# Wave 0 reordered, the second half of wave 1 transposed by the DMA crossbar, wave 2's loads strung out behind it and its work two steps later, in a fused linear-attention and MLP kernel

## The chip, the cores and the metric

One core of one Trainium2 chip. The metric is the time of one execution on the device in microseconds (us). A profile's span is some 2 us shorter than the time of the same execution. Most executions of a kernel agree within about 1%; a state is given where a run fell out of line ("slow", more than 1.5% above the fastest of the same kernel).

## The reference

Linear attention with decay over blocks of 64 positions (4 batches, 8 heads, 768 positions, head size 64), then an MLP (512 to 2048 to 512, 3072 tokens) with a GELU in its sigmoid form. All inputs and the output are float32.

```python
for b in range(nb):
    sl = slice(b * block, (b + 1) * block)
    qb, kb, vb = (q[:, :, sl], k[:, :, sl], v[:, :, sl])
    intra = np.einsum('bhic,bhjc->bhij', qb, kb) * Dmask[None]
    intra = np.einsum('bhij,bhjd->bhid', intra, vb)
    inter = np.einsum('bhid,bhde->bhie', qb * lam_pow[None], kv_state)
    out[:, :, sl] = intra + inter
    kb_dec = kb * rev_pow[None]
    kv_state = lam_block[None, :, None, None] * kv_state + np.einsum('bhsd,bhse->bhde', kb_dec, vb)
# x: the heads side by side, (3072, 512)
h = x @ w_in
g = h * (1.0 / (1.0 + np.exp(-1.702 * h)))
return (g @ w_out).astype(np.float32)
```

## The kernel before

The tokens are worked off in six waves of 512. Waves 0 and 1 are cut into "units" (two batches and a pair of heads; the units of wave 1 come in two halves, A and B), waves 2 to 5 into pairs of heads. For each, k and q are scaled and cast to bf16 (the tile `kqs`, by DVE and POOL), transposed (`kq`), multiplied to scores (`ps_s`), masked, and turned into an output, which is transposed once more into `xT`, the input of the MLP's first matmul (`ps_h`). A KV state is carried from wave to wave.

A list of main work (MLP matmuls, 0.216 us for 512 columns) carries a clock; attention work is slotted in by time on that clock. This order is the order of the program; each engine works through its own part of it in that order.

```python
def u_turn(w, bl, p):                      # waves 0 and 1: transposed by TensorE
    t = ps.tile([P, 8, P], bf16, ...)
    for i in range(2):
        for j in range(2):
            nc.tensor.transpose(t_ps[w, bl, p][:, i, j, :], kqs_of[w, p][:, bl, i, j]..., ident)

def p_cast(w, p):                          # waves 2 to 5: cast, then transposed by the crossbar
    ...
    nc.sync.dma_start_transpose(out=kq_of[w, p]..., in_=kqs...)

def p_out(w, p):
    ...
    nc.scalar.copy(xs.rearrange("s b h d -> s h b d"), o)
    nc.sync.dma_start_transpose(out=xT(w)[:, p], in_=xs.rearrange("p b h d -> p (b h d)"))

# ... loads of waves 0 and 1 and of both weights are queued here, on SyncE (SP) ...
load_batches(2)                            # all 12 loads of wave 2, right behind them
pump()                                     # issues what the ring of staging buffers has room for

# ... wave 0: for each unit transposes, inter and out of an older unit, scores of the last ...

e = clock[0]                               # start of wave 0's second matmul
# ... 16 steps of wave 0's output ...
states(e - 7, 0, 1.6)
units1(e + 2, B_UNITS, 2, nc.scalar, nc.scalar)
e = clock[0]
# ... 8 steps of wave 1's second half, 16 steps of its output ...
full(e + 1, e + 7.6, 2, 2.4)               # wave 2: casts from e + 1, scores from e + 7.6
load_spread(e + 4, 3, 1.8)                 # wave 3's loads, one at a time
```

## Time and profile before

| | before |
|---|---|
| time, median (range) | 220.36 us (220.35 to 221.56) |
| span of the profiled execution | 218.7 us |
| TensorE busy | 207.8 us (95%) |
| TensorE's waits behind 24 us | 0.7 us in total at most for any one cause |
| first matmul of wave 2's MLP | 92.78 us, without a wait |

The page's rows of the 40 slices (5.5 us each), here the bytes moved, show one thing that the prediction passed over: between 44 and 66 us, the ninth to twelfth slices, the DMA engines move 200 to 276 GB/s. Most of these bytes are wave 2's loads (twelve of 256 KB, 3.1 MB of some 5.0).

```profile
GB/s 137 295 290 364 342 315 389 362 276 201 218 222 86 145 242 167 225 242 221 207 171 186 233 161 227 134 147 192 236 151 73 46 74 83 88 0 0 48 51 96
```

### The profile page before, as it was taken

Reading aid. Unit: us, or ns where it says so; the run is one execution under the profiler, and the core shown is the slowest. Engines: PE = TensorE matmul, PEld = TensorE weight load, DVE = VectorE, ACT = ScalarE, POOL = GpSimd, SP = SyncE. Lnnn points to the kernel's source line nnn. Section 1 sums busy time; section 2 is a strip of 40 time slices with the busy share of each in tenths; the row PEclk is TensorE's granted clock in tenths of the full one; section 3 lists DMA queues with packets and bytes.
Section 4 is the critical chain, followed back from the end, with each engine's and each line's share of the span. In section 5 each row is a group of like instructions: output and inputs, shape, how many; then the busy total and the mean of one; then the engine's idle time right before and its main releaser. Section 6 shows DMA issues by size and latency. Waiting matters only on the chain.

```text
span 218.7 us, 4482 instructions
## 1 busy us (share of the span) xinstructions
PE 207.8 (95%) x1745; PEld 108.6 (50%) x1772; DVE 105.2 (48%) x237; ACT 97.4 (45%) x203; POOL 30.3 (14%) x62
## 2 busy tenths in 40 slices
PE   7887999899999999999999999999999999999993
PEld 2454454574547755444554444544444454444452
DVE  2577736595316888193572294661484332100121
ACT  5476867773655611156611075611176420376000
POOL 8780052041021000004000040000040000000000
PEclk9999999999999999999999999999999999999999
DMA  4999999999994999999989979667973222200112
GB/s 137 295 290 364 342 315 389 362 276 201 218 222 86 145 242 167 225 242 221 207 171 186 233 161 227 134 147 192 236 151 73 46 74 83 88 0 0 48 51 96
DMA packets 96741, 40.15 MB, mean 184 GB/s; under 512 B 77136, under 2 KB 89680, under 8 KB 96720
## 3 DMA queue, kind: packets, MB, share of 16 engines
q1 hardware_dynamic: 96576, 39.86, 76.5%
q8 instruction: 14, 0.23, 0.4%
q14 instruction: 7, 0.06, 0.1%
q10 hardware_dynamic: 144, 0.00, 0.0%
HBM read 27.27 MB, written 6.29 MB: 153 GB/s over the span
## 4 chain that ended last, share of the span: by engine, by line
PE 84%; DVE 4%; ACT 4%; DMA 2%; issue 2%; SPq 1%; POOL 1%
PE ps_h L450 35%; PE ps_out L481 35%; PE ps_o L431 2%; PE ps_s L394 2%; DMA ring<-in_q_dram 2%; DVE w_out L150 2%; PE ps_out L497 2%; SPq L89 1%; ACT kv_bd L335 1%; PE ps_kv L409 1%; PE ps_o L369 1%; PE ps_o L424 1%; PE ps_t L280 1%; PE ps_o L360 1%; PE ps_s L301 1%
## 5 line engine op out<-in xcount | busy, mean ns | idle before, releaser
L450 PE MATMUL ps_h<-xT,w_in 128*128 128x512 bf16 (+1 forms) x438 | 87.1, 348 | 1.3 <-ACT g_sb L456 0.7
L456 ACT ACTIVATE g_sb<-ps_h 128x512 bf16<-128x512 f32 (+1 forms) x112 | 59.6, 536 | 57.6 <-PE ps_h L450 56.2
L481 PE MATMUL ps_out<-w_out,g_sb 128*128 128x512 bf16 x354 | 80.8, 379 | 0.8 <-issue 0.3
L450 PEld LDWEIGHTS <-w_in 128*128 128x128 bf16 x448 | 42.2, 98 | 38.5 <-issue 1.1
L481 PEld LDWEIGHTS <-g_sb 128*128 128x128 bf16 x368 | 34.8, 98 | 38.9
L488 DVE COPY o_sb<-ps_out 128x512 f32<-128x512 f32 x19 | 13.1, 691 | 52.6 <-PE ps_out L481 47.1
L401 DVE SCALAR_TENSOR_TENSOR sm<-ps_s,inv_pow,mask 128x512 bf16<-128x512 f32 x32 | 22.6, 747 | 22.9 <-PE ps_s L394 22.8
L383 POOL CAST v_sb<-ring 128x512 bf16<-128x512 f32 x16 | 9.8, 656 | 102.1 <-DMA ring<-in_v_dram 68.0
L434 ACT CAST xs<-ps_o 128x512 bf16<-128x512 f32 x16 | 9.4, 586 | 29.2 <-PE ps_o L431 29.2
L306 DVE TENSOR_TENSOR sm<-ps_s,mask 128x512 bf16<-128x512 f32 x16 | 11.0, 689 | 11.9 <-PE ps_s L301 11.9
L263 POOL TENSOR_TENSOR kqs<-ring,kq_pow 128x256 bf16<-128x256 f32 x16 | 10.3, 652 | 27.9 <-DMA ring<-in_q_dram 27.8
L413 DVE SCALAR_TENSOR_TENSOR kv<-kv,blk,ps_kv 64x256 bf16<-64x256 bf16 x24 | 11.4, 475 | 0.2
L381 DVE TENSOR_SCALAR kqs<-ring,k_pow 128x256 bf16<-128x256 f32 x32 | 11.2, 391 | 0.2
L381 DVE TENSOR_SCALAR kqs<-ring,q_pow 128x256 bf16<-128x256 f32 x32 | 11.1, 390 | 0.0
L288 ACT COPY kq<-ps_t 128x512 bf16<-128x512 bf16 x12 | 7.0, 586 | 9.1 <-PE ps_t L280 9.0
L255 PE MATMUL ps_f<-zeros 128*128 128x512 bf16 x25 | 9.3, 506 | 1.7 <-DVE zeros L178 1.3
L263 DVE TENSOR_TENSOR kqs<-ring,kq_pow 128x256 bf16<-128x256 f32 x16 | 7.5, 474 | 5.5 <-DMA ring<-in_k_dram 3.0
L350 DVE TENSOR_TENSOR kv<-kv_bd,ps_kv 64x128 bf16<-64x128 bf16 x16 | 4.6, 286 | 8.2 <-PE ps_kv L347 7.9
L371 ACT CAST xT<-ps_o 128x256 bf16<-128x256 f32 x16 | 6.0, 373 | 3.6 <-PE ps_o L369 3.5
L280 PEld LDWEIGHTS <-kqs 128*128 128x128 bf16 x64 | 4.7, 98 | 5.7 <-DVE kqs L263 1.9
L280 PE MATMUL ps_t<-ident,kqs 128*128 128x128 bf16 x64 | 6.4, 220 | 1.0 <-POOL kqs L263 0.7
L150 DVE CAST w_out<-ring 128x512 bf16<-128x512 f32 x16 | 7.1, 498 | 0.1
(66 smaller groups left out, 117.8 us busy)
## 6 DMA issues: line engine op xcount, KB each, us to landing
ring<-in_k_dram SPq DMA_DIRECT2D x23, 256.0 KB, 4.9
ring<-in_q_dram SPq DMA_DIRECT2D x23, 256.0 KB, 4.4
ring<-in_v_dram SPq DMA_DIRECT2D x23, 256.0 KB, 4.5
ring<-in_moe_w_in_dram SPq DMA_DIRECT2D x16, 256.0 KB, 5.9
ring<-in_moe_w_out_dram SPq DMA_DIRECT2D x16, 256.0 KB, 5.4
out_dram<-o_sb SPq DMA_DIRECT2D x15, 256.0 KB, 2.2
out_dram<-o_sb SPq DMA_DIRECT2D x18, 128.0 KB, 2.6
ring<-in_k_dram SPq DMA_DIRECT2D x2, 128.0 KB, 3.2
```

Of the source, the lines that this page charges most:

```text
L150: eng.tensor_copy((w_in_sb if kind == "in" else w_out_sb)[j][:, r, :], read(kind, j, r))
L263: eng.tensor_tensor(kqs_of[w, p][:, bl, i].rearrange("s j h d -> s h j d"), read(w, "kq"[i], bl, p), tab, op=MUL)
L280: nc.tensor.transpose(t_ps[w, bl, p][:, i, j, :], kqs_of[w, p][:, bl, i, j].rearrange("s h d -> s (h d)"), ident)
L306: nc.vector.tensor_tensor(sm.rearrange("s h j t -> s h (j t)"), s_ps.pop((w, bl, p))[:, :, 0 : 2 * P], mask2.to_broadcast([P, 2, 2 * P]), ...
L381: nc.vector.tensor_scalar(kqs[:, i, :, h, :], x[:, :, p, h, :], scalar1=(k_pow, q_pow)[i][:, 2 * p + h : 2 * p + h + 1], scalar2=None, op0 ...
L383: nc.gpsimd.tensor_copy(v_sb[w % 2][:, p], read(w, "v")[:, :, p])
L401: nc.vector.scalar_tensor_tensor(sm[:, h], s[:, h], inv_pow[:, 2 * p + h : 2 * p + h + 1], mask.to_broadcast([P, B, P]), op0=MUL, op1=MUL)
L413: nc.vector.scalar_tensor_tensor(new[hd(h), p], old[hd(h), p], blk2[hd(h), p : p + 1], t[hd(h), :, hd(h)], op0=MUL, op1=ADD)
L450: nc.tensor.matmul(t[:, bs[0] * P : bs[1] * P], w_in_sb[fc // CW][:, kc, (fc % CW) * P : (fc % CW + 1) * P], xT(w)[:, kc, bs[0] : bs[1], : ...
L456: nc.scalar.activation(g_tile(w)[:, fc, c], h_ps.pop((w, fc))[:, c], GELU)
L481: nc.tensor.matmul(t, g_of[w][:, fc, g * P : (g + 1) * P], w_out_sb[j][:, fc % CW, :], start=(fc == 0), stop=(fc == FFC - 1))
L488: nc.vector.tensor_copy(o, t)
```

## The change

Its intent: in the head, open the circle of waits in wave 0 (scores first, so that the scaling of the KV state isn't waited for), one filler matmul less a unit, the GELU table loaded early, some first loads issued by ACT, three slices of w_in cast by POOL. In wave 1's second half, take 16 transposes off TensorE. To keep the queue clear for those crossbar transposes, wave 2's loads are strung out behind them; and wave 2's casts and scores move two steps (1.7 us) later. The core of the diff, cuts marked:

```diff
+    for p in range(2):
+        load_units(0, "k", 0, p, 1)
+        load_units(0, "q", 0, p, 1, nc.scalar)
 ...
-    load_batches(2)
     pump()
 ...
+    nc.scalar.activation(warm, inv_pow[:, 0:1], GELU)      # the table, early
 ...
+    def u_xbar(w, bl, p):
+        nc.sync.dma_start_transpose(out=kq_of[w, p][:, bl]..., in_=kqs_of[w, p][:, bl]...)
 ...
-                nc.vector.tensor_copy(o[:, 0 : hw // 2], t[:, 0 : hw // 2])
-                nc.scalar.copy(o[:, hw // 2 :], t[:, hw // 2 :])
+                nc.scalar.copy(o, t)                       # the last half of the output
 ...
-    FILL0, FILL1 = 12, 2
+    FILL0, FILL1 = 12, 1
 ...
-        nc.gpsimd.memset(blk_bd, 0.0)                      # before the loop over units
+            if i == 1:                                     # in the loop, ahead of the casts
+                nc.gpsimd.memset(blk_bd, 0.0)
 ...
-            if u2:
-                u_inter(0, *u2)
-            if u:
-                u_turn_copy(0, *u, nc.scalar)
-            if u2:
-                u_out(0, *u2)
             if u1:
                 u_score(0, *u1)
                 u_kv0(0, *u1)
                 ...
+            if u2:
+                u_inter(0, *u2)
+                u_out(0, *u2)
 ...
+        def units1b(t_cast, t0, c_step, step):
+            for i in range(n):
+                at(t_cast + c_step * i, u_cast_kq, 1, 0, *u, nc.vector)
+                at(t_cast + c_step * i, u_cast_kq, 1, 1, *u, nc.gpsimd)
+                at(t_cast + c_step * i, u_xbar, 1, *u)
 ...
-        units1(e + 2, B_UNITS, 2, nc.scalar, nc.scalar)
+        units1b(e + 3.4, e + 8.5, 1.2, 1.6)
+        load_spread(e + 4, 2, 1.15)
 ...
-        full(e + 1, e + 7.6, 2, 2.4)
+        full(e + 3, e + 9.6, 2, 2.4)
```

More of the change, by code (lines that the diff above doesn't have):

```diff
@@ L84, with load_units @@
     head, used, where, coming = [0], set(), {}, []
-    def load_units(w, nm, bl, p, n=2):
+    def load_units(w, nm, bl, p, n=2, queue=nc.sync):
         def go(x):
-            nc.sync.dma_start(
+            queue.dma_start(
                 out=x.rearrange("s (h c) -> s h c", h=2 * n),
@@ L103, in load_batch @@
         coming.append((2 * B if b == 0 else 0, [(w, nm)] if b == 0 else [], NP, go))
-    def load_batches(w):
-        for nm in "kqv":
-            for b in range(B):
-                load_batch(w, nm, b)
     def load_w(kind, j, r):
@@ L159 @@
     UNITS = [(bl, p) for g in range(2) for bl in range(2) for p in (2 * g, 2 * g + 1)]
-    LOADS0 = [(0, 0, 1), (0, 1, 1), (1, 0, 2), (0, 2, 2), (1, 2, 2)]
+    LOADS0 = [(1, 0, 2), (0, 2, 2), (1, 2, 2)]
     A_UNITS, B_UNITS = [(0, p) for p in range(NP)], [(1, p) for p in range(NP)]
+    for p in range(2):
+        load_units(0, "k", 0, p, 1)
+        load_units(0, "q", 0, p, 1, nc.scalar)
+    load_units(0, "v", 0, 0)
     for bl, p, n in LOADS0:
@@ L206 @@
     kq_pow2 = const.tile([P, 2, NP, 2, 2], f32)
-    for j in range(2):
-        for i in range(2):
+    for i in range(2):
+        for j in range(2):
             nc.scalar.activation(kq_pow2[:, i, :, :, j], ln_lam.rearrange("s (p h) -> s p h", h=2), EXP,
@@ L290, in u_turn_copy @@
             eng.tensor_copy(out, t)
+    def u_xbar(w, bl, p):
+        nc.sync.dma_start_transpose(out=kq_of[w, p][:, bl].rearrange("p i j s -> p (i j) s"),
+                                    in_=kqs_of[w, p][:, bl].rearrange("p i j h d -> p (i j h d)"))
     s_ps = {}
@@ L446, in mlp1 @@
         if (w, fc) not in h_ps:
-            h_ps[w, fc] = ps.tile([P, W], f32, tag="mm", bufs=3, name="ps_h")
+            if (w, fc) == (0, NF):
+                h_ps[w, fc] = ps.tile([P, 2, W], f32, tag="s", name="ps_h4")[:, 0, :]
+            else:
+                h_ps[w, fc] = ps.tile([P, W], f32, tag="mm", bufs=3, name="ps_h")
         t = h_ps[w, fc]
@@ L503, in mlp2_last @@
             else:
-                nc.vector.tensor_copy(o[:, 0 : hw // 2], t[:, 0 : hw // 2])
-                nc.scalar.copy(o[:, hw // 2 :], t[:, hw // 2 :])
+                nc.scalar.copy(o, t)
             store(w, g, o, slice(c * hw, (c + 1) * hw))
-    FILL0, FILL1 = 12, 2
+    FILL0, FILL1 = 12, 1
+    NF = 3
     A_T, A_S = 6, 1.4
+    KV_ENG = {i: nc.vector if i in (2, 4, 6) else nc.scalar for i in range(1, 9)}
     with tc.manual_schedule():
@@ L514 @@
         blk_bd = const.tile([P, NP, 2, D], f32)
-        nc.gpsimd.memset(blk_bd, 0.0)
-        for h in range(2):
-            nc.gpsimd.tensor_copy(blk_bd[hd(h), :, h, :],
-                                  blk2[hd(h)].rearrange("s (p d) -> s p d", d=1).to_broadcast([64, NP, D]))
         N = len(UNITS)
@@ L526 @@
             u2 = UNITS[i - 2] if 1 < i else None
+            if i % 2 and u:
+                u_cast_v(0, *u, nc.gpsimd)
+            if i == 1:
+                nc.gpsimd.memset(blk_bd, 0.0)
+                for h in range(2):
+                    nc.gpsimd.tensor_copy(blk_bd[hd(h), :, h, :],
+                                          blk2[hd(h)].rearrange("s (p d) -> s p d", d=1).to_broadcast([64, NP, D]))
             if i + 1 < N:
@@ L529 @@
                 u_cast_kq(0, 1, *UNITS[i + 1], nc.gpsimd)
-            if u:
+            if i % 2 == 0 and u:
                 u_cast_v(0, *u, nc.gpsimd)
+            if i == N - 1:
+                for r in range(3):
+                    cast_w("in", *ROWS[r], nc.gpsimd)
             if u:
@@ L534 @@
                 u_turn(0, *u)
-            if u2:
-                u_inter(0, *u2)
-            if u:
-                u_turn_copy(0, *u, nc.scalar)
-            if u2:
-                u_out(0, *u2)
+                u_turn_copy(0, *u, nc.vector if i < 2 else nc.scalar)
+            if i == N:
+                for fc in range(NF):
+                    mlp1(0, fc, [0])
             if u1:
@@ L543 @@
                 u_kv0(0, *u1)
-                if i == N:
-                    cast_w("in", *ROWS[0], nc.vector)
                 u_mask(0, *u1)
-                u_kv0_copy(0, *u1, nc.vector if i % 2 else nc.scalar)
-                if i == N:
-                    cast_w("in", *ROWS[1], nc.vector)
+                u_kv0_copy(0, *u1, KV_ENG[i])
+            if u2:
+                u_inter(0, *u2)
+                u_out(0, *u2)
             pump()
-            if i == N + 1:
-                nc.scalar.activation(warm, q_pow[:, 0:1], GELU)
             if i >= N:
-                for fc in range(3):
-                    mlp1(0, fc, [i - N])
-        for u in ROWS[2:]:
+                for fc in range(NF):
+                    mlp1(0, fc, [i - N + 1])
+        for u in ROWS[3:]:
             cast_w("in", *u, nc.vector)
             pump()
-        for kc in range(2, KC):
-            for fc in range(3):
-                mlp1(0, fc, [kc])
-        for fc in range(3):
+        for fc in range(NF):
+            mlp1(0, fc, [3])
             gelu(0, fc)
@@ L600, in units1 @@
                     at(h, u_kv0_copy, 1, *units[i - 1], nc.scalar)
+        def units1b(t_cast, t0, c_step, step):
+            n = len(B_UNITS)
+            for i in range(n):
+                u = B_UNITS[i]
+                at(t_cast + c_step * i, u_cast_kq, 1, 0, *u, nc.vector)
+                at(t_cast + c_step * i, u_cast_kq, 1, 1, *u, nc.gpsimd)
+                at(t_cast + c_step * i, u_xbar, 1, *u)
+                at(t_cast + c_step * i, u_cast_v, 1, *u, nc.gpsimd)
+            for i in range(n + 1):
+                t = t0 + step * i
+                at(t, new_o)
+                if i < n:
+                    at(t, u_score, 1, *B_UNITS[i])
+                    at(t, u_mask, 1, *B_UNITS[i])
+                if i:
+                    at(t, u_inter, 1, *B_UNITS[i - 1])
+                if i < n:
+                    at(t, u_kv0, 1, *B_UNITS[i])
+                if i:
+                    at(t, u_out, 1, *B_UNITS[i - 1])
+                if i < n:
+                    at(t, u_kv0_copy, 1, *B_UNITS[i], nc.scalar)
         def states(t0, w, step):
@@ L625 @@
         HA, HB = (0, 2), (2, 4)
-        for fc in range(3, FFC):
+        for fc in range(NF, FFC):
             put(1, fc_whole, 0, fc)
```

## The prediction

> **What bounds the kernel now.** I read the page first (busy shares and the 40 slices), then the chain of waits in order of time, then busy times by stage, then the timeline around the places where the chain leaves TensorE.
>
> ```profile
> PE 207.8 (95%) x1745; PEld 108.6 (50%) x1772; DVE 105.2 (48%) x237; ACT 97.4 (45%) x203; POOL 30.3 (14%) x62
> DMA  4999999999994999999989979667973222200112
> PE 84%; DVE 4%; ACT 4%; DMA 2%; issue 2%; SPq 1%; POOL 1%
> ```
> TensorE carries 84% of the chain. The DMA row is as important: from the second slice (5.5 us) to the twelfth (about 65 us) the 16 DMA engines are saturated. So there are two limits in the first 65 us, and only TensorE afterwards.
>
> How full is TensorE? In the chain a 512-column matmul costs 0.216 us (47 in 10.14 us at 201.50), a 256-column one 0.118 (12 in 1.42), a unit of wave 0 or 1 about 0.95 (transposes 0.22, scores 0.24, output 0.25, KV and inter matmuls the rest), a pair of waves 2 to 5 about 1.1 (0.33 + 0.22 + 0.56). From 24.00 to 215.4 there are 676 full matmuls (146.0), 128 halves (15.1), the last 32 halves (3.67), 8 units (7.6), 8 states of 0.25 (2.0) and 16 pairs (16.8, the last four without KV): 191.2 us in 191.4. Behind 24 us TensorE has almost no gap; only removing its work, or starting earlier, helps there. The head is where it has gaps:
>
> ```profile
> 0.00:9.00 9.00, 7.73 (x40) 3.23 (x40) 2.94 (x12) 4.69 (x14) 6.53 (x21) 1.00 0.70 199
> 9.00:24.00 15.00, 11.32 (x197) 6.76 (x201) 11.75 (x28) 10.67 (x26) 6.74 (x13) 1.00 1.01 327
> 24.00:30.00 6.00, 6.00 (x28) 2.74 (x28) 2.67 (x7) 4.51 (x8) 0.61 (x1) 1.00 1.11 319
> ```
> Columns: stretch, length, busy time of PE, weight loads, DVE, ACT, POOL, clock, DMA share, GB/s. From 9 to 24 us no engine is full, but the DMA share is already 1.01. The chain there goes round in circles of 1.58 us a unit and ends in a table load:
>
> ```profile
> 20.36 0.31 ACT kv_bd L335
> 20.69 0.32 ACT kv_bd L335
> 21.06 0.23 PE ps_o L360
> 21.29 0.27 PE ps_o L369 x8
> 21.58 0.37 ACT xT L371
> 21.97 1.28 ACT L552
> 23.26 0.20 ACT warm L552
> 23.46 0.49 ACT g_sb L456
> 24.00 6.20 PE ps_h L450 x28
> ```
> The reader is to see that ACT scales the KV state just before TensorE needs it, and that the GELU table is loaded when the first GELU waits for it. The last thing I looked at is the next meeting of TensorE with new data, the first transpose of wave 1 (three rows of the timeline of all engines, 28.2 to 30.2 us):
>
> ```profile
> 28.28 0.42 DVE L263 TENSOR_TENSOR kqs<-ring,kq_pow 128x256 bf16<-128x256 f32 x1 [0.47 <-DMA ring<-in_k_dram]
> 29.21 0.61 POOL L263 TENSOR_TENSOR kqs<-ring,kq_pow 128x256 bf16<-128x256 f32 x1 [12.38 <-DMA ring<-in_q_dram]
> 29.83 0.42 PEld L280 LDWEIGHTS <-kqs 128*128 128x128 bf16 x4
> ```
> POOL starts the moment the load of q lands (29.2), and TensorE the moment POOL is done (29.83). This handover already has no slack. The four last slices of w_in also find DVE waiting for DMA (four waits, 1.4 us).
>
> **What the Trainium skill says.** "DMA: Bandwidth & Descriptors", section "Issuing engines are not separate DMA queues": a second issuing engine saves only the time on the sequencer, the transfers share the same 16 engines. The trace before has 0.46 to 0.51 us of SP per issue in the first 5 us, and 280 to 300 GB/s already in the stretch from 3 to 9 us; so I expect little from ACT's two issues. "ScalarE: Activation LUTs", "What ACT_TABLE_LOAD costs": about 1283 ns for the load, plus a drain. The trace agrees on the load (1.28); the drain of 1.38 us isn't seen, the next ACT instruction starts at once. "TensorE: Matmul & The Clock Gate", "What's actually happening": after about 3.4 us of idleness the array falls to half rate, and needs as long again of work to come back. The trace agrees at the start (14 fillers in 5.80 us, 0.41 each against 0.216 later); no later idle stretch is long enough to test it.
>
> **The change part by part.**
>
> Head. (a) Scores now come ahead of inter and output within a unit, so the KV scaling has a whole unit's time instead of being waited for: the 1.58 us circle opens. What is left per unit: ACT 0.59 (copy of k, q) + 0.37 (xT) + 0.64 in five of eight = 1.2 to 1.3 us on the mean; DVE 0.43 to 0.69 + 0.69 + some 0.28 = about 1.25; POOL 0.61 + 0.5 = 1.1. I take 1.3, so about 0.28 x 8 = 2.2 us less. (b) Eight fewer fillers (in the first group cold, 0.43, later 0.22) and the earlier first POOL cast: 0.4 us at the start. (c) The table load of 1.28 and its warm-up of 0.20 move to about 6 us, where ACT is idle: 1.5 us less. (d) POOL casts three w_in slices before the last unit (0.66 each), the fourth accumulator (borrowed from the scores) lets fc 3 run ahead of the first GELU: about 0.4 us. Sum: TensorE would be at the first wave 1 transpose 2.2 + 0.4 + 1.5 + 0.4 = 4.5 us sooner, at about 25.3 instead of 29.83.
>
> But what that transpose needs hasn't moved as much. Wave 0's q, k, v (3.15 MB), w_in (4.19 MB) and wave 1's first k, q stand in the same order in the same queue, each load waiting for the one eight before it. By 10 us the stream had moved 2.07 MB; with ACT issuing and v fetched in one piece I give it the saturated 0.29 MB per us from 2.3 us on, so 2.23 MB: 0.16 MB, or 0.5 us, and up to 0.3 more from fewer issue gaps. Estimate: q lands 0.8 us sooner, at 28.4, plus POOL's 0.61: transpose at 29.0. So TensorE gives back about 3.7 of its 4.5 us in one wait. **Head: -0.8 us.**
>
> Wave 1, second half. 16 transposes leave TensorE: four groups, on the chain 0.40 + 0.22 + 0.22 + 0.22 = 1.06 us. ACT loses four copies of 0.59 and four v casts of 0.40. In their place four crossbar transposes, each half as large as those of waves 2 to 5, which take 3.6 us from issue to landing under load. Casts stand at 3.4 and scores at 8.5 of the schedule's clock (a step is 4 matmuls, 0.864 us): 4.4 us between them, less 0.6 to 1.1 for the casts, so 3.3 us or more. Enough, if wave 2's loads, which are now strung out behind the transposes, don't fill the queue. Units now follow at 1.6 steps instead of 2, so ACT's xT 0.37 + scaling 0.64 may hold TensorE for 0.1 or 0.2 us two or three times: +0.3. **Net -0.8 us.** Spreading wave 2's loads itself removes no wait of TensorE; wave 2's first scores move two steps later and other matmuls fill the place: 0.
>
> Tail. The last half was copied by DVE (0.29) and then ACT (0.27), one after the other because both write one tile; ACT alone takes 256 columns in 0.37 (as its xT copies). **-0.2 us.**
>
> Sum: 0.8 + 0.8 + 0.2 = 1.8 us, and 220.4 - 1.8 = 218.6; I also hold 0.2 us more likely from the smoother queue than against it, and say **218.4 us**, 0.9% faster.
>
> **The rivals.** First: the loads aren't the limit, and the head gives its full 4.5 us; then 220.4 - 4.5 - 1.0 = 214.9 (2.5% faster). For it: TensorE's gaps in the head are real, and GB/s in 14 to 18 us dips to 269 and 332, so the stream has some slack. Against it: the DMA share of 1.0 to 1.1 without a break to 53 us, and POOL starting at the landing. Second: the new wait at the first wave 1 transpose lasts 3 to 4 us, just the length at which the array falls to half rate; then 3.4 us of work at half speed cost up to 1.7 us and the change ends at 220. For it: the length. Against it: the free-running window must fall wholly into the gap. Third: a crossbar transpose lands late among the loads and TensorE waits for wave 1's scores; with landing at 5 us instead of 3.6 each of the first units waits about 1 us, and the change comes to 219.5. Against it: the queue is less full there, as wave 2's loads stand behind each transpose.
>
> **Range and chances.** Without the array cooling and with transposes in time the time is 217.5 to 218.8, depending on the stream (0.3 to 1.7 us sooner). Half a chance in three for one of the slower rivals takes it to 219.9; a tenth for the first rival, wholly or in large part, takes it below 216. So 8 in 10 between 216.3 and 219.9; faster by over 2% (below 215.95) 0.11, within 2% 0.86, slower 0.03.
>
> **What would show it.** In the changed kernel's chain: units of wave 0 about 1.3 us apart; no table load between the last xT and the first GELU; the last w_in slices still found by DVE at their landing near 26.5; then a wait of TensorE of 3 to 4 us ended by POOL's q cast for wave 1 near 29. If that wait is under 1 us, the first rival is right and the stream was not the limit. If matmuls after it last 0.43 us, the second is. If the second half of wave 1 shows TensorE waiting for a DMA into kq, the third is. From wave 2 on the chain should be the same, shifted; any difference there makes my account wrong. The tail should show one ACT copy of 0.37.

## More of the kernel before

Every load, every store and every crossbar transpose is issued by SP.

SP's part of the timeline gives their issue (start, length of the group, engine and line, operation, tile and source, count). Twelve loads go out one behind another from 44.49 to 59.8 us.

```profile
44.49 6.34 SPq L101 DMA_DIRECT2D ring<-in_k_dram  x4
50.92 3.81 SPq L101 DMA_DIRECT2D ring<-in_q_dram  x4
54.83 4.98 SPq L101 DMA_DIRECT2D ring<-in_v_dram  x4
```

## The result, and the profile after

| | before | after |
|---|---|---|
| median of 4 runs (range) | 220.62 us (220.35 to 221.56) | 227.28 us (226.38 to 228.43) |
| ratio of fast runs, 95% interval | | 1.0297 (1.0236 to 1.0357) |
| span of the profiled execution | 218.7 us | 224.9 us |
| granted clock, mean | 0.999 | 0.985 |

Ratios here and below are the mean time of one kernel's fast runs over that of the other's of the same rounds, so not quite the ratio of the medians. The change is 3.0% slower. The prediction said 0.9% faster, and its range ended at 219.9.

Where does TensorE lose the 6.2 us? I laid the same matmuls of the two timelines side by side:

| the first matmul of ... | before | after | difference |
|---|---|---|---|
| wave 1's first transposes | 30.04 | 29.65 | -0.39 |
| wave 0's output | 48.64 | 48.28 | -0.36 |
| wave 1's second half, hidden layer | 66.32 | 65.83 | -0.49 |
| wave 2's hidden layer | 92.78 | 95.05 | +2.27 |
| wave 3's scores | 101.50 | 108.11 | +6.61 |
| end of the span | 218.7 | 224.9 | +6.2 |

So the change is half a microsecond ahead at 66 us, and loses 7.1 us in the next 42. At 66 us it has a third of the 1.6 us that the prediction gave it up to there; the loss lies where I had written 0. (The part before 66 us came about in another way than foretold; that is taken up below.)

The busy times by stage show the end of this stretch, 95 to 102 us (columns: stretch, its length, busy time of PE, weight loads, DVE, ACT, POOL, clock, DMA share, GB/s). In the changed kernel:

```profile
95.00:98.30 3.30, 0.86 (x4) 0.29 (x3) 2.96 (x10) 0.00 (x0) 0.00 (x0) 1.00 0.77 199
98.30:102.00 3.70, 3.44 (x9) 1.34 (x10) 2.02 (x8) 1.19 (x2) 0.00 (x0) 0.54 0.92 219
```

TensorE is idle for 2.44 of these 3.3 us, in one wait of 2.5, and then the granted clock is 0.54 for 3.7 us: 3.7 x 0.46 = 1.7 us lost to the cold array. Which waits there are, the list of waits of the changed kernel says (engine, tile and line <- what ended the wait: us in total, times, longest; DVE's, SP's and PE's lines picked out):

```profile
SPq L293 <- DVE kqs L262: 7.8, 1, 7.8
...
PE ps_h L457 <- DMA xT<-xs: 2.5, 1, 2.5
...
PE ps_s L398 <- DMA kq<-kqs: 1.9, 1, 1.9
...
PE ps_kv L351 <- DVE kv L354: 0.7, 1, 0.7
```

The three waits of PE didn't exist before. Their sum, 5.1, with the 1.7 of the cold array and 0.2 of issue behind the last wait makes 7.0, of the 7.1 that are lost between 66 and 108 us. So the loss is found; what is its cause?

The first line is the answer. SP stands still for 7.8 us at line 293, the first crossbar transpose of wave 1's second half. Its timeline (compare the twelve loads of before):

```profile
42.85 0.70 SPq L89 DMA_DIRECT2D ring<-in_v_dram  x1
51.39 1.29 SPq L293 DMA_TRANSPOSE kq<-kqs  x1
52.74 0.57 SPq L101 DMA_DIRECT2D ring<-in_k_dram  x1
```

Nothing is issued from 43.6 to 51.4 us. The transpose waits for DVE's cast of `kqs`, and DVE does that at 50.92, behind its last six casts of w_out (48.06 to 51.0). In the kernel before wave 2's loads were issued just then, from 44.49. In the changed one they stand behind the transpose in the program of SP, and an issue that waits holds up all issues behind it. The page's row of bytes moved shows what is not moved: 89 and 98 GB/s in the ninth and tenth slices, where it was 276 and 201.

```profile
GB/s 148 292 343 378 330 323 396 329 89 98 213 234 222 193 205 239 190 231 203 216 92 171 184 230 196 175 119 196 196 217 107 28 50 113 96 0 0 37 56 93
```

Wave 2's loads are then issued from 52.7 to 72.2 us, 12 us later at their end, and meet stores of wave 0 on the way that wait as well. The chain of waits of the changed kernel tells how this reaches TensorE (start, us, what; line 478 is the store, 385 the cast of q):

```profile
64.51 0.48 SPq L478
...
65.03 1.49 SPq L478
...
66.56 4.04 DMA ring<-in_q_dram
...
74.91 6.24 DMA kq<-kqs
...
95.46 2.83 DMA xT<-xs
...
98.34 1.30 PE ps_h L457 x3
```

A store waits for its data, a load of q stands behind it and lands at 70.6; DVE waits for it (its cast of wave 2 stands ahead of wave 1's KV state, hence TensorE's 0.7 us there); the cast, and with it the crossbar transposes of wave 2, come late (issued 72.3 to 81.4, before 69.1 to 76.1) and, among the late loads, take 5.0 us to land instead of 3.6 (medians of four each); TensorE waits 1.9 us for the second; and the last `xT` is issued at 95.46, where it was 89.43. That last step has two more parts, which the trace shows. ACT's last cast into `xs` waited 2.65 us for one of the two `xs` buffers, until an earlier transpose out of it landed at 91.91. And the cast was done at 92.60, but SP issued its transpose only at 95.46, behind the third transpose, a load and two stores.

### The profile page after: what moved, and what is told of

Same layout as the page of the kernel before. It is cut to its first block, busy times and chain, and to the rows that moved or that the text cites. A ratio compares the mean times of both kernels' runs of the same rounds, so it can differ in the third digit from the quotient of the medians.

```text
span 224.9 us, 4426 instructions
## 1 busy us (share of the span) xinstructions
PE 209.7 (93%) x1721; PEld 108.1 (48%) x1748; DVE 103.1 (46%) x234; ACT 93.8 (42%) x195; POOL 35.8 (16%) x69
## 4 chain that ended last, share of the span: by engine, by line
PE 79%; DMA 9%; ACT 3%; SPq 3%; issue 2%; POOL 2%; DVE 1%; DVEq 0%; ACTq 0%; POOLq 0%
PE ps_h L457 35%; PE ps_out L488 29%; DMA xT<-xs 3%; DMA kq<-kqs 3%; PE ps_o L435 2%; PE ps_s L398 2%; DMA ring<-in_q_dram 2%; DMA lam_p<-in_lam_dram 2%; PE ps_s L305 2%; PE ps_t L279 2%; PE ps_out L504 2%; SPq L478 1%; PE ps_o L373 1%; PE ps_kv L413 1%; POOL kqs L262 1%
## 5 line engine op out<-in xcount | busy, mean ns | idle before, releaser
L457 PE MATMUL ps_h<-xT,w_in 128*128 128x512 bf16 (+1 forms) x438 | 88.6, 352 | 3.6 <-DMA xT<-xs 2.5
L387 POOL CAST v_sb<-ring 128x512 bf16<-128x512 f32 x16 | 11.7, 768 | 108.8 <-DMA ring<-in_v_dram 82.6
L385 DVE TENSOR_SCALAR kqs<-ring,q_pow 128x256 bf16<-128x256 f32 x32 | 10.5, 369 | 1.1 <-DMA ring<-in_q_dram 1.1
L385 DVE TENSOR_SCALAR kqs<-ring,k_pow 128x256 bf16<-128x256 f32 x32 | 10.5, 370 | 0.2
L279 PE MATMUL ps_t<-ident,kqs 128*128 128x128 bf16 x48 | 5.6, 236 | 3.2 <-POOL kqs L262 2.4
L254 PE MATMUL ps_f<-zeros 128*128 128x512 bf16 x17 | 7.2, 566 | 1.3 <-DVE zeros L176 1.3
L398 PE MATMUL ps_s<-kq 64*128 64x128 bf16 x128 | 6.4, 219 | 2.1 <-DMA kq<-kqs 1.9
L339 ACT ACTIVATE kv_bd<-ps_o,blk 64x64 bf16<-64x64 f32 x16 | 4.9, 309 | 8.0 <-PE ps_o L330 7.7
L398 PEld LDWEIGHTS <-kq 64*128 64x128 bf16 x128 | 3.6, 94 | 8.8 <-issue 5.9
```

Of the source, the lines that this page charges most:

```text
L385: nc.vector.tensor_scalar(kqs[:, i, :, h, :], x[:, :, p, h, :], scalar1=(k_pow, q_pow)[i][:, 2 * p + h : 2 * p + h + 1], scalar2=None, op0 ...
L387: nc.gpsimd.tensor_copy(v_sb[w % 2][:, p], read(w, "v")[:, :, p])
L398: nc.tensor.matmul(s[:, h, b, :], t[hd(h), 0, b, :], t[hd(h), 1, b, :], start=True, stop=True)
L457: nc.tensor.matmul(t[:, bs[0] * P : bs[1] * P], w_in_sb[fc // CW][:, kc, (fc % CW) * P : (fc % CW + 1) * P], xT(w)[:, kc, bs[0] : bs[1], : ...
```

## The experiments

Twelve kernels were run, each several times against the kernel before on the same chip. Where nothing else is said, the state is fast. In the diffs `# ...` and ` ...` mark what is left out.

**1. The head alone.** The kernel before with the new wave 0, new order of loads and table load; transposes, wave 2's loads, shift and tail as before.

```diff
  # against the changed kernel
+    load_batches(2)
-        units1b(e + 3.4, e + 8.5, 1.2, 1.6)
-        load_spread(e + 4, 2, 1.15)
+        units1(e + 2, B_UNITS, 2, nc.scalar, nc.scalar)
-        full(e + 3, e + 9.6, 2, 2.4)
+        full(e + 1, e + 7.6, 2, 2.4)
 ...                                   # load_batches itself, and the tail's two copies
```

> Wave 0's new order, fillers, w_in casts on POOL and early table load alone; wave 1's second half, wave 2's loads and the tail as before. My theory (the loss is made behind 66 us, the head is a wash because POOL's late q cast and a cold array give its gain back): first transpose of wave 1 at 29.2 to 29.9 us, total within 1 us of the kernel before, 219.7 to 221.2. Rival (the head's cold stretches and its later order do the harm): 223 us or more.

Measured: 220.47 us against 220.73; ratio 0.9975 (0.9917 to 1.0032). Its profile fell in a slow run (223.8 us, clock 0.969) and is not used for times. The head is neither gain nor loss within the interval; the loss is elsewhere. (Its fastest runs took 220.34 us at a clock of 0.999 and 220.31 at 0.992, so a lower mean clock costs nothing here that can be seen.)

**2. The rear alone.** The kernel before with crossbar transposes, strung-out loads and the shift.

```diff
  # against the kernel before
-    load_batches(2)
-        units1(e + 2, B_UNITS, 2, nc.scalar, nc.scalar)
+        units1b(e + 3.4, e + 8.5, 1.2, 1.6)
+        load_spread(e + 4, 2, 1.15)
-        full(e + 1, e + 7.6, 2, 2.4)
+        full(e + 3, e + 9.6, 2, 2.4)
 ...                                   # u_xbar and units1b themselves
```

> Wave 0 and the tail as before; only the crossbar transposes of wave 1's second half, the strung-out loads of wave 2 and the two steps' later wave 2. My theory: the whole loss is here, 225.5 to 228 us, with SP standing still until about 51 us before its first crossbar transpose and the DMA queue under 100 GB/s from 48 to 56 us. Rival (head and rear each do part): 222 to 224.

Measured: 226.78 us; ratio 1.026 (1.0206 to 1.0313). Within the intervals the whole loss is here. Its stretch of 50 to 56 us shows the same hole in the loads (DMA share 0.30, 64 GB/s), and its list of waits the same two waits of TensorE, 1.1 us for `kq` and 2.7 for `xT`. The stretch:

```profile
50.00:56.00 6.00, 6.00 (x29) 2.74 (x28) 3.11 (x8) 0.00 (x0) 0.82 (x2) 1.00 0.30 64
```

**3. The transposes back on TensorE, the loads still strung out.** If the crossbar's wait alone held the loads, taking it away should give the loads back.

```diff
  # against the changed kernel
-        units1b(e + 3.4, e + 8.5, 1.2, 1.6)
+        units1(e + 2, B_UNITS, 2, nc.scalar, nc.scalar)
         load_spread(e + 4, 2, 1.15)
```

> The changed kernel, but wave 1's second half is transposed by TensorE again as before; wave 2's loads stay strung out in the program and wave 2 stays two steps later. My theory (the loads are late only because SP issues in order and the crossbar transposes ahead of them wait for DVE): with that transpose no longer ahead the loads go out early again, 219.5 to 221.5. But four transposes by DMA still stand between the loads in the order of the program, so it isn't this run if they aren't removed; they are. Rival (stringing the loads out, or starting wave 2 two steps later, is itself the loss): 225 or more.

Measured: 227.77 us (224.66 to 230.29), ratio of the two fast runs 1.021 (1.0116 to 1.0304), so whether it is over 2% is unclear. Not the recovery that I expected. The profile, of a slow run, so good for the order of things and not for times, says why: without a transpose to wait for, SP waits for the next thing in its program, a store of wave 0 that stands among the strung-out loads, and for longer.

```profile
49.40 0.74 SPq L101 DMA_DIRECT2D ring<-in_q_dram  x1
63.88 2.13 SPq L478 DMA_DIRECT2D out_dram<-o_sb  x2
```

From 56 to 60 us not a byte moves:

```profile
56.00:60.00 4.00, 4.00 (x54) 2.26 (x53) 1.50 (x3) 2.28 (x6) 0.00 (x0) 1.00 0.00 0
```

So the crossbar transpose is one thing that can hold the loads, and a store is another. (This run keeps the shift too, which has a cost of its own, see experiment 5.)

**4. The loads first.** Wave 2's loads close together and mostly ahead of the transposes, shift kept.

```diff
  # against the changed kernel
-        load_spread(e + 4, 2, 1.15)
+        load_spread(e + 1.5, 2, 0.5)
```

> The changed kernel with the crossbar transposes kept, but wave 2's twelve loads put earlier in the program: all of k stands in SP's queue ahead of the first crossbar transpose, q and v between the following ones. My theory: SP issues k before it waits for DVE, most of the loss goes: 219.5 to 222. Rival (crossbar transposes cost the time themselves, or collide with the loads): 224 or more, with TensorE waiting for kq of wave 1.

Measured: 228.28 us; ratio 1.0313 (1.0241 to 1.0385). A miss. The k loads do go out from 44.45 as before, but the transposes, now between q and v loads, land late, and TensorE waits for them, 1.02 and 1.04 us, and cools (clock 0.83 in 56 to 66 us). And the wait for `xT` is there in full, though wave 2's loads are early:

```profile
PE ps_h L457 <- DMA xT<-xs: 2.6, 1, 2.6
...
PE ps_s L305 <- DMA kq<-kqs: 2.1, 2, 1.0
```

That pointed to the two-step shift as a cause by itself, the part that I had priced at 0.

**5. The shift alone.** One line of the kernel before.

```diff
  # against the kernel before
-        full(e + 1, e + 7.6, 2, 2.4)
+        full(e + 3, e + 9.6, 2, 2.4)
```

> The kernel before with one edit: wave 2's casts and scores stand two steps (1.7 us of matmuls) later in the program. My theory (the last transpose of wave 2's output landed with no slack before wave 2's first matmul, so every step later is a wait of TensorE[...]): 222 to 224.5, with a wait of 1.5 to 2.5 us for xT near 95 us. Rival (the shift is free, as I predicted, and only the late loads cost): within 0.5 us of before.

Measured: 222.93 us; ratio 1.0103 (1.0055 to 1.0151); span 220.9, 2.2 longer than before. TensorE's timeline there:

```profile
92.56 0.81 PE L450 MATMUL ps_h<-xT,w_in 128*128 128x512 bf16 x3
95.59 8.14 PE L450 MATMUL ps_h<-xT,w_in 128*128 128x512 bf16 x37 [2.22 <-DMA xT<-xs]
```

One new wait of 2.22 us, and the span is 2.2 longer: the shift is a cost of its own. In the kernel before, the last `xT` landed at 92.7, and the fourth matmul, the first to read it, came at about 93.4: 0.7 us to spare. I had expected the array to cool as well; this wait did not cool it (clock 0.999).

The last `xT` is issued 3.2 us later than before (92.64 against 89.43), more than the shift of 1.7. The cast into `xs` that it waits for ends at 89.94, 1.5 us later (88.43 before). The rest is SP's order again: before, SP issued the transpose 1.0 us after the cast; here it came 2.7 us after it, since the third transpose, a load and two stores now stood ahead of it:

```profile
90.69 0.59 SPq L101 DMA_DIRECT2D ring<-in_v_dram  x1
91.38 1.16 SPq L471 DMA_DIRECT2D out_dram<-o_sb  x2
92.64 1.24 SPq L435 DMA_TRANSPOSE xT<-xs  x1
```

So about half of the shift's delay is later work and half the place in SP's queue. The shift with this transpose moved ahead of the load and the stores was not run.

**6. The loads first, without the shift.**

```diff
  # against experiment 4
-        full(e + 3, e + 9.6, 2, 2.4)
+        full(e + 1, e + 7.6, 2, 2.4)
```

> The changed kernel with both edits at the rear: wave 2's loads ahead in the queue, and wave 2's casts and scores back at their old steps. My theory (two separate losses, late loads and the shift): the wait for xT falls under 0.5 us and the time to 221 to 223.5; what is left over 220.5 is the wait for wave 1's crossbar transposes behind the loads (about 2 us in the run before) and the cold array after it. Rival (the crossbar costs more than both): still over 225.

Measured: 222.7 us; ratio 1.009 (1.0041 to 1.014). The wait for `xT` is gone (the first 40 matmuls of wave 2's MLP run from 94.50 without a stop), and three waits for wave 1's `kq`, 2.1 us together, are what remains. Compared with experiment 4, the shift costs 2.2% in this company (1.0313 - 1.009), more than alone. Experiment 4's profile has two cold stretches that this one lacks: 1.7 us behind the wait for `xT` (clock 0.75 in 98.3 to 105 us) and 1.7 us at 56 to 66, which has nothing to do with the shift.

**7. The head with POOL's table moved.** In the changed kernel's head POOL builds `blk_bd` just ahead of the q cast for which TensorE waits. Here it is built two units later, and DVE's turns at scaling the KV state start later too. Nothing else is changed from experiment 1.

```diff
  # against experiment 1
-    KV_ENG = {i: nc.vector if i in (2, 4, 6) else nc.scalar for i in range(1, 9)}
+    KV_ENG = {i: nc.vector if i in (4, 6, 8) else nc.scalar for i in range(1, 9)}
-            if i == 1:
+            if i == 3:
                 nc.gpsimd.memset(blk_bd, 0.0)
```

> The new head alone, but POOL builds the block table two units later, so it stands no longer ahead of the third unit's q cast. My theory: TensorE's 2 us wait near 9 us shrinks to under 0.7, the array stays warm, TensorE reaches wave 1's first transpose 2 us sooner and then waits there for the load of q, which lands at 28.6 or so: total 219.5 to 220.5, so at most 1 us better than before. Rival (that load isn't a limit): 218.5 or less.

Measured: 220.21 us against 220.99; ratio 0.9992 (0.9944 to 1.004). The profiled run has its clock at 0.999, so the head's cold stretch is gone; TensorE is at wave 1's first transposes at 27.86, 2.2 us earlier than before, and there it waits for POOL's cast of q:

```profile
27.86 0.28 PE L285 MATMUL ps_t<-ident,kqs 128*128 128x128 bf16 x2
28.92 0.29 PE L285 MATMUL ps_t<-ident,kqs 128*128 128x128 bf16 x2 [0.78 <-POOL kqs L268]
```

The head, mended, gives most of its gain back at the loads, as the prediction said of the unmended one: POOL's cast starts when q lands, at 28.25, and the lead over the kernel before is down to 0.8 us at the fourth group of transposes (33.05 against 33.86) and at wave 0's output (47.83 against 48.64). That is what I had predicted for the head, 0.8; in the times it stays within the interval.

**8. Wave 1's first loads ahead of the last four slices of w_in.** If the place of q in the queue were the limit, moving it up should keep the gain.

```diff
  # against experiment 7
-    for u in ROWS:
+    for u in ROWS[:12]:
         load_w("in", *u)
 ...
+            for u in ROWS[12:]:           # behind wave 1's first loads
+                load_w("in", *u)
 ...
+        for n, u in enumerate(ROWS[12:]):
+            at(8.0 + 0.1 * n, cast_w, "in", *u, nc.vector)
```

> The run before plus one edit to the loads and the new tail: wave 1's first half is loaded ahead of the last four w_in slices, whose casts stand later in DVE's order. My theory (the order of the loads is the head's limit): the first transpose of wave 1 starts near 26.5 us instead of 29.2, and the total is 217 to 218.5, better than both kernels. Rival (another limit follows at once, w_in's last slices or DVE): 219.5 or more, with TensorE waiting for w_in near 30 us.

(It also has the new tail.) Measured: 220.98 us; ratio 1.0005 (0.995 to 1.006). My theory missed, the rival held. The wait moved to the slices of w_in that now come later:

```profile
PE ps_h L465 <- DVE w_in L150: 2.0, 4, 0.9
```

DVE, which casts them, itself waits 1.4 us for the load of w_in at 30.5. I take it that all of these bytes are needed by about 31 us, in whichever order, and that the order only chooses who waits. The profiled run also cooled behind these waits (clock 0.53 to 0.62 in 34 to 38 us); the two runs with a clock of 0.997 or more took 219.94 and 220.04 us, which is still above the 217 to 218.5 expected.

**9. The changed kernel without the shift.**

```diff
  # against the changed kernel
-        full(e + 3, e + 9.6, 2, 2.4)
+        full(e + 1, e + 7.6, 2, 2.4)
```

> The changed kernel with only the shift of wave 2 undone; its loads stay late. My theory (the two losses lie in series: wave 2's first scores can't come sooner than its late loads allow, so undoing the shift alone brings less than the 2.2 us that the shift costs alone): 225 to 227, with TensorE waiting for kq of wave 2 near 75 to 80 us. Rival (the losses simply add): 224.3 to 225, and the wait for xT gone.

Measured: 223.36 us against 221.13; ratio 1.0123 (1.0081 to 1.0166), less than I expected, and less than the rival's 224.3; the wait for wave 2's `kq` that I expected isn't there. Late loads without the shift cost 1.2%; TensorE waits 0.8 us for `xT` and 1.6 for the KV state, and the clock is 1.00 from 95 to 105 us. SP's wait at the first crossbar transpose is still 7.6 us.

**10. The crossbar alone.** All twelve loads of wave 2 ahead, no shift.

```diff
  # against the kernel before
-        units1(e + 2, B_UNITS, 2, nc.scalar, nc.scalar)
+        units1b(e + 3.4, e + 8.5, 1.2, 1.6)
 ...                                   # u_xbar and units1b themselves
```

> The kernel before with only wave 1's second half moved to the crossbar: wave 2's loads all stand ahead of the transposes as they did before, wave 2 at its old steps. My theory (SP issues in order, so the transposes wait behind twelve loads until about 60 us while TensorE wants the first near 56): TensorE waits 4 to 7 us for kq of wave 1, 224 to 228. Rival (transposes pass the loads): 219.5 to 220.5.

Measured: 228.76 us; ratio 1.0353 (1.0332 to 1.0373), slightly over the range expected. The transposes queue behind the twelve loads, SP issues the first at 58.89, TensorE waits for it and then runs cold (clock 0.66 in 60 to 70 us):

```profile
PE ps_s L306 <- DMA kq<-kqs: 6.1, 1, 6.1
```

So the reason for stringing out the loads is sound: with the loads ahead, this wait would be there. One in-order queue serves two customers, and each can hold up the other.

**11. Four k loads, then the four transposes, then the rest**, the head of experiment 7, no shift.

```diff
  # against experiment 9, besides the head of experiment 7
-        load_spread(e + 4, 2, 1.15)
+        for i in range(3 * B):
+            at(e + (1.5 + 0.4 * i if i < B else 7.2 + 0.4 * (i - B)), load_batch, 2, "kqv"[i // B], i % B)
```

> An attempt at a better version: the changed kernel with POOL's block table later, wave 2's k ahead of the four crossbar transposes, its q and v behind them without stores between, and wave 2 at its old steps. My theory: no wait for kq of wave 1 over 0.3 us, q landed by about 66 us, 218.8 to 220.3. Rival (q is still too late for wave 2): 221.5 or more with a wait for kq or xT of wave 2.

Measured: 221.88 us against 221.13; ratio 1.0046 (1.0014 to 1.0077). The best of the versions with the crossbar; SP's wait is down to 1.8 us, no wait for wave 1's `kq`, 0.8 us each for `xT` and the KV state. Still no gain; this is nearer to the rival.

**12. Casts and transposes earlier**, the head of experiment 7, no shift. If DVE's late cast is what holds SP, an earlier one frees it.

```diff
  # against experiment 9, besides the head of experiment 7
-        units1b(e + 3.4, e + 8.5, 1.2, 1.6)
-        load_spread(e + 4, 2, 1.15)
+        units1b(e - 2.0, e + 8.5, 0.8, 1.6)
+        load_spread(e - 1.5, 2, 0.8)
```

> The changed kernel with POOL's block table later and wave 2 at its old steps, as in the run before, and with DVE's casts for the crossbar moved five steps up, between w_out's casts, each crossbar transpose followed by one load of k, then q and v without stores between. My theory (SP's wait for DVE ahead of its first crossbar transpose is what makes the loads late): SP issues the first one near 47 us instead of 51.4, the DMA queue no longer falls under 100 GB/s between 48 and 56 us, no wait of TensorE for kq, and the only gain left is the removed transposes: 219 to 220.3 against 220.7 to 221.0 before. Rival (other handovers of the rear, DVE's order above all, keep the time up): 221 to 222.

Measured: 222.7 us against 220.91; ratio 1.0094 (1.0058 to 1.013). 5.4 steps (4.7 us) earlier in the program made the first transpose only 3.2 us earlier on the chip, at 48.16, because DVE comes to its cast at 47.55, behind other work in its order; SP still waits 3.3 us for it. TensorE waits 1.9 us for `xT`. A miss, and above the rival's range as well. No version beats the kernel before; experiment 7 equals it within its interval.

## Why the prediction was wrong

**The step that failed** was "Spreading wave 2's loads itself removes no wait of TensorE; wave 2's first scores move two steps later and other matmuls fill the place: 0." Both halves of it were wrong. In their place the runs showed:

- The shift costs 2.2 us by itself (experiment 5). Other matmuls do fill the place of the scores, but what hangs on the scores, the last `xT`, had only 0.7 us to spare in the kernel before (issued at 89.43, landed at 92.7, first read at about 93.4). The shift delayed its issue by 3.2 us, half of it because a load and two stores came ahead of it in SP's order. I followed the work that TensorE does, not the chain that hangs on it.
- Late loads cost some 1.2%, 2.7 us (experiment 9; the head in it is worth 0 by experiment 1), net of the little that the crossbar and the tail bring. They are late because SP issues in the order of its program, and the first crossbar transpose waits 7.8 us in it. I had asked whether the loads would delay the transposes, not whether the transposes would delay the loads. That was in reach without a run: on the program's clock the transpose stands at 3.4 and the first load at 4, and DVE's casts of w_out at this place are in the profile of before.
- Together they cost 2.97%, against 1.23 + 1.03. The difference of 0.7% is not clear of noise (by the three intervals it is 0.7 give or take 0.9). In the profiled executions it is 1.2 us (6.2 against 2.2 + 2.8), and there the changed kernel has a cold array (1.7 us) behind its wait of 2.48 us that neither experiment 5 (a wait of 2.22, clock 0.999) nor 9 (0.8) has at this place. I take the cold array for the difference; it was not tried by itself.
- The sign that I had named for the rest, a chain that is the same from wave 2 on, failed for these reasons.

**The head: -0.8 predicted, about -0.4 in the profile, 0 within the interval (experiment 1).** The predicted 4.5 us of TensorE's time did not come, so there was nothing to hand back. The table load did leave the chain (1.5 us). But the stretches of the head in the changed kernel read so:

```profile
9.00:11.00 2.00, 0.18 (x2) 0.11 (x2) 0.81 (x2) 0.15 (x1) 1.80 (x5) 1.00 1.17 290
...
13.00:15.00 2.00, 2.00 (x34) 1.17 (x26) 1.52 (x3) 1.58 (x5) 2.00 (x5) 0.54 1.06 340
```

TensorE idles for 2 us; its clock stays at 1.00 for two more (11 to 13 us) and is then 0.54 to 0.60 for some 4 us. The wait ends with POOL's third cast of q, ahead of which POOL built a table:

```profile
8.56 0.52 POOL L534 MEMSET blk_bd<- 128x512 f32 x1
...
9.14 0.93 POOL L536 COPY blk_bd<-blk 64x256 f32<-64x256 f32 x2
...
10.82 0.28 PE L279 MATMUL ps_t<-ident,kqs 128*128 128x128 bf16 x2 [1.96 <-POOL kqs L262]
```

Before, the same table was made at 5.14, ahead of the first cast, and POOL still had 1.43 us to spare before the third. From the second unit's scores (11.04) to the last (20.37) a unit took 9.33 / 6 = 1.56 us, not the 1.3 that I gave it. (In experiment 7, units without a wait do follow at 1.29: their scores start at 13.21, 14.50 and 15.79.) Experiment 7 moves the table (and the turns of DVE with it), and the cold stretch and the wait of 2 us are gone. The two edits were not tried apart, but the order on POOL is what the trace shows ahead of the wait; I had read over those moved lines of the diff.

**The DMA stream as the head's limit: right for the mended head.** The load of q landed at 28.61, 0.6 us sooner than before (predicted 0.8, at 28.4). In the changed kernel TensorE comes too late to wait for it, so the wait of 3 to 4 us which I named as the sign is not there, and taken literally my sign would have spoken for the first rival, wrongly:

```profile
28.61 0.61 POOL L262 TENSOR_TENSOR kqs<-ring,kq_pow 128x256 bf16<-128x256 f32 x1 [10.50 <-DMA ring<-in_q_dram]
...
29.65 0.39 PE L279 MATMUL ps_t<-ident,kqs 128*128 128x128 bf16 x4
```

Experiments 7 and 8 show the limit: with a better head TensorE waits for q, and with q moved up it waits for w_in.

**Wave 1's second half: -0.8 predicted, -0.13 measured** (65.83 - 48.28 = 17.55, before 17.68). The 1.06 us of transposes did leave TensorE, and the four crossbar transposes landed in time (2.6 to 3.1 us), as predicted. The rest of the term was mis-sized: the hold-ups of the shorter pitch, put at 0.3, must be some 0.9 if the removed 1.06 is right; I did not break them down.

**The tail: right.** One ACT copy of 0.37 us ends the kernel where DVE's 0.29 and ACT's 0.27 stood.

**The rivals.** The first (the head's full gain) is refuted. The second named the right mechanism, the array going cold, at the wrong place; what I held against it, that the window must fall wholly into the gap of 3 to 4 us, did not help, as the array cooled behind waits of 1.96 and 2.48 us. The third, a crossbar transpose that lands late, came true for wave 2's transposes, not wave 1's: TensorE waits 1.9 us for one. No rival had a load that is late because its issue waits; the range, which ended at 219.9, had no room for it. The chance of slower by over 2% was put at 0.03.

## What to carry to other kernels

SP issued its DMAs in the order of its program here, and each one that waited held up the rest (7.8 us in the changed kernel, 6.1 us of TensorE in experiment 10): for each issue you move, ask what it will wait for and which loads stand behind it, since spacing in the program is not spacing in time. Before moving a stage later, find the last thing that hangs on it and how much slack that has, not only whether the engine has other work meanwhile. A wait can cost more than its length: behind the one of 2.48 us the array ran at a clock of 0.54, 1.7 us more. Not tried here: giving part of these issues to another engine than SP, and a third `xs` buffer.

## What the Trainium skill lacked or had wrong

- "DMA: Bandwidth & Descriptors", section "Issuing engines are not separate DMA queues", says that a second issuing engine saves only time on the sequencer, usually small. Agreed for the head, where ACT's two issues and v in one piece brought q 0.6 us sooner. But the section leaves out the case: an issue that waits blocks the sequencer for all behind it, 7.8 us in the changed kernel and 13.7 us in experiment 3 (50.1 to 63.9, in a slow run), and that was not small beside a load's 4 to 5 us.
- "DMA: Bandwidth & Descriptors", section "DMA Transpose (X-bar)", gives constraints and no latency under load, nor does another page. Here a transpose of wave 2 took 3.6 us from issue to landing (3.1 to 4.7) in the kernel before and 5.0 (3.9 to 6.2) where loads crowd it; the half-size ones of wave 1 took 2.6 to 3.1 on an emptier queue.
- "TensorE: Matmul & The Clock Gate", section "What's actually happening", puts the fall to half rate at one idle window of about 3.4 us. In the changed kernel the clock fell to 0.54 behind one wait of 2.48 us (98.3 us), and in 13 to 15 us with no idle stretch before it but one of 1.96 us that had ended at 10.82. In experiment 4 two waits of 1.02 and 1.04 us were enough (0.50 to 0.53 in 62 to 65 us). A wait of 2.22 us in experiment 5 left the clock at 0.999, and three of 0.64, 1.05 and 0.41 in experiment 6 left it at 1.00. So waits well below 3.4 us can cool the array, not all do, and the length alone doesn't tell which. The way back also took longer at the start than the 3.4 us that the prediction took from the page: the fillers stayed at 0.43 us each from 1.25 to 6.35, 5.1 us of work.
- "ScalarE: Activation LUTs", section "What ACT_TABLE_LOAD costs", adds a drain of about 1380 ns to the load of 1283. The load was 1.28 us here; the next ACT instruction started 0.01 us after it (6.85 + 1.28, next at 8.14) and the one before it had ended at 6.83, so no drain was seen.
